# Fused attention and feed-forward kernel: chunk 2's q and k transposed on TensorE, chunk 1 prepared after product 1, attention 1 started ahead of product 2

## The chip, the cores and the metric

The kernel runs on one NeuronCore of a Trainium2 chip. The metric is the device time of one execution in microseconds (us). Before the change three runs gave 260.45, 261.06 and 263.18 us; the median is 261.06.

## The reference, cut to what matters

```python
# q, k, v: (4, 8, 768, 64) float32; three of the eight heads are "retrieval" heads
scores = q @ k.T / 8                      # per batch and head
mask = causal                             # retrieval heads 0, 2, 6
mask = causal & (key < 4 | query - key < 64)   # the five other (streaming) heads
a = softmax(where(mask, scores, -1e9)); attn = a @ v
x = attn.transpose(0, 2, 1, 3).reshape(3072, 512)
h = x @ w_in                              # (512, 2048)
out = maximum(0.01 * h, h) @ w_out        # (2048, 512), float32
```

## The kernel before, in words

The 3072 tokens are cut into eight chunks of 384 (two per batch, `n = 0 .. 7`). A chunk passes through four stages. Its q, k and v come from DRAM by GpSimd's DMAs, cast to bfloat16 on the way (`load`, L78), 256 bytes of DRAM per head and token. Its q and k are transposed so that the head dimension lies on the partitions (`kt`, `qt`). Then comes attention (`Attention`, L276), whose result `xs` is transposed again to `xt`. Then the two feed-forward products: product 1 (`in_slots`, L451) makes `g` from `xt` in 16 ticks of four matmuls and one ScalarE activation, and product 2 (`out_slots`, L463) makes three output tiles from `g` in 16 slots, each tile copied from PSUM by VectorE and stored by SyncE's queue.

There are two ways to transpose. Chunks 0 and 1 do it on TensorE: `prep_pair(n, p)` (L193) transposes one pair of heads with six 128x128 transposes into one PSUM bank, and VectorE copies them out, two halves to `kt` and one tile to `qt`. Chunks from `BY_DMA` = 2 on do it with the DMA crossbar: `prep_dma(n)` (L216) issues six `dma_start_transpose` on SyncE's queue, three for k (from `kz`, a copy of k with zeroed halves) and three for q. The `xt` of chunks 0 to 2 is made on TensorE (`x_t`, L408, three transposes and one ScalarE copy for each pair of heads); from chunk 3 on it is a crossbar transpose issued from `finish` (L404).

The order of each engine's work is the order in which the program is written (`manual_schedule`); nothing is rescheduled. Stages are interleaved by hand: `merge(ms, as_)` (L494) spreads the list `as_` over the list `ms`. Attention is a list of slots; slot t computes the scores of unit t, and the product with v of unit t-2. Product 1 of chunk 0 starts at L542; L543 to L546 put the four pairs of chunk 1 behind its first seven ticks. L551 merges the last five ticks with the first eight slots of attention 1, and then product 2 of chunk 0 with the rest. L560 merges both products of chunk 1 with attention 2. The loop from L563 merges product 1 of chunk n, product 2 of chunk n-1 (from n = 3 on) and attention n+1.

GpSimd's DMAs are issued in program order and use eight completion semaphores in turn, so each issue waits until the DMA issued eight earlier has landed. SyncE's queue is also in program order: vb copies (`v_shift`), crossbar transposes and output stores wait behind each other. PSUM has eight banks: two each for the tags `ph`, `psS` and `po`, one each for `py` and `pt`.

Of the kernel before, what the change touches and what calls it, by code (L numbers as in the profile page):

```python
# [21 lines left out]
def kernel(  # L22
# [13 lines left out]
    B, H, S, D = q.shape  # L36
# [8 lines left out]
    KG = DM // 128  # L45
    NCH = B * (S // CH)

    BY_DMA = 2

    ctx.enter_context(tc.manual_schedule())  # L50
    one = ctx.enter_context(tc.tile_pool(name="one", bufs=1))
# [5 lines left out]
    def bank(tag, shape, dtype):  # L57
        return ps.tile(shape, dtype, name=tag, tag=tag, bufs=BANKS[tag])
# [19 lines left out]
    def load(n, nms="kqv"):  # L78

        b, c = divmod(n, 2)  # L80
        for nm in nms:
            if nm == "k" and n >= BY_DMA:

                for g in range(3):
                    for hh in range(2):
                        nc.gpsimd.dma_start(out=kz[n % 2][:, g, hh::2, D * hh : D * hh + D],  # L86
                                            in_=nat[nm][b, c, :, hh::2, g])
                continue
            if nm != "v":
                cast[nm, n] = rot.tile([128, 3, H, D], BF16, name=f"{nm}b", tag=f"{nm}b", bufs=2)  # L90
            for g in range(3):
                o = va[b % 2][:, 3 * c + g, :, 0:D] if nm == "v" else cast[nm, n][:, g]
                nc.gpsimd.dma_start(out=o, in_=nat[nm][b, c, :, :, g])  # L93

    def load_w(which, i):

        if which == "in":
            c = slice(512 * i, 512 * i + 512)
            nc.gpsimd.dma_start(out=w_in_bf[:, :, c], in_=w_in_r[:, :, c])
        else:  # L100
            c = slice(4 * i, 4 * i + 4)
            nc.gpsimd.dma_start(out=w_out_bf[:, c, :], in_=w_out_r[:, c, :])
# [27 lines left out]
    def zeros(i, c):  # L130
        t = slice(CH * c, CH * c + CH)
        nc.vector.memset(kt[i][64:128, :, 0, t], 0.0)
        nc.vector.memset(kt[i][0:64, :, 1, t], 0.0)

    def zeros_k(i):
        nc.vector.memset(kz[i][:, :, 0::2, D:], 0.0)
        nc.vector.memset(kz[i][:, :, 1::2, 0:D], 0.0)
# [48 lines left out]
    def sink_keys(n, p, hh):  # L186
        b, c = divmod(n, 2)
        h = 2 * p + hh
        if c == 0 and not IS_RETR[h]:
            r = slice(64 * hh, 64 * hh + 64)  # L190
            nc.vector.tensor_copy(ksink[b % 2][r, p, NS * h : NS * h + NS], kt[b % 2][r, p, hh, 0:NS])

    def prep_pair(n, p, tag="pt", eng=("v", "v", "v")):  # L193
        b, c = divmod(n, 2)
        i = b % 2
        if p == 0:
            qts[n] = rot.tile([128, 4, CH], BF16, name="qt", tag="qt", bufs=2)
        pt = bank(tag, [128, 2, 4, 128], BF16)
        for e, nm in enumerate("kq"):
            for g in range(3):  # L200
                nc.tensor.transpose(pt[:, e, g, :], cast[nm, n][:, g, 2 * p : 2 * p + 2, :], ident[:])

        def move(e, dst, src):
            dst = dst.rearrange("p (g t) -> p g t", g=3)
            if e == "v":
                nc.vector.tensor_copy(dst, src)
            else:
                nc.scalar.activation(out=dst, in_=src, func=ACTF.Copy)

        for hh in range(2):  # L210
            r = slice(64 * hh, 64 * hh + 64)
            move(eng[hh], kt[i][r, p, hh, CH * c : CH * c + CH], pt[r, 0, 0:3, :])
            sink_keys(n, p, hh)
        move(eng[2], qts[n][:, p, :], pt[:, 1, 0:3, :])

    def prep_dma(n):  # L216
        b, c = divmod(n, 2)
        i = b % 2
        qts[n] = rot.tile([128, 4, CH], BF16, name="qt", tag="qt", bufs=2)
        for g in range(3):  # L220
            t = slice(128 * g, 128 * g + 128)
            tk = slice(CH * c + 128 * g, CH * c + 128 * g + 128)
            nc.sync.dma_start_transpose(out=kt[i].rearrange("p a e t -> p (a e) t")[:, :, tk],
                                        in_=kz[n % 2][:, g].rearrange("p h d -> p (h d)"))
            nc.sync.dma_start_transpose(out=qts[n][:, :, t], in_=cast["q", n][:, g].rearrange("p h d -> p (h d)"))
# [223 lines left out]
    py = {}  # L449

    def in_slots(n, tags=("ph",)):  # L451
        def tick(t):
            if t == 0:
                gs[n] = rot.tile([128, NG, CH], BF16, name="g", tag="g", bufs=2)
            ph = bank(tags[t % len(tags)], [128, 512], FP32)
            for g in range(KG):
                nc.tensor.matmul(ph[:, 0:CH], lhsT=w_in_bf[:, g, 128 * t : 128 * t + 128],  # L457
                                 rhs=xts[n][:, g, :], start=(g == 0), stop=(g == KG - 1))
            nc.scalar.activation(out=gs[n][:, t, :], in_=ph[:, 0:CH], func=ACTF.Prelu, alpha=0.01)  # L459

        return [lambda t=t: tick(t) for t in range(NG)]

    def out_slots(n, tags=("py", "py", "py"), halves=False):  # L463
        slots = []

        def part(tt, lo, hi, tag, c0, c1):
            if lo == 0:
                py[n] = bank(tag, [128, 512], FP32)
            for ng in range(lo, hi):
                nc.tensor.matmul(py[n][:, 0 : c1 - c0], lhsT=gs[n][:, ng, 128 * tt : 128 * tt + 128],  # L470
                                 rhs=w_out_bf[:, ng, c0:c1], start=(ng == 0), stop=(ng == NG - 1))
            if hi == NG:
                o = rot.tile([128, DM], FP32, name="o", tag="o", bufs=3)
                r0 = CH * n + 128 * tt
                nc.vector.tensor_copy(o[:, 0 : c1 - c0], py[n][:, 0 : c1 - c0])  # L475
                nc.sync.dma_start(out=out[r0 : r0 + 128, c0:c1], in_=o[:, 0 : c1 - c0])

        for tt in range(3):
            if halves and tt == 2:
                slots.append(lambda: part(2, 0, NG, "py", 0, 256))  # L480
                slots.append(lambda: part(2, 0, NG, "psS", 256, 512))
                continue
            lo = 0
            for w in ([3, 3, 3, 3, 4], [3, 3, 3, 3, 4], [3, 3, 3, 3, 2, 2])[tt]:
                slots.append(lambda tt=tt, lo=lo, w=w: part(tt, lo, lo + w, tags[tt], 0, DM))
                lo += w
        return slots

    def run(*lists):
        for l in lists:  # L490
            for f in l:
                f()

    def merge(ms, as_):  # L494

        r, done = [], 0
        for j, m in enumerate(ms):
            want = (j + 1) * len(as_) // len(ms)
            r += as_[done:want] + [m]
            done = want  # L500
        return r + as_[done:]

    def preps(n):
        return [lambda p=p: prep_pair(n, p) for p in range(4)]
# [13 lines left out]
    load(0, "v")  # L518
    load_vb0()
    masks()  # L520
    for i in range(3):
        load_w("in", i)
    load(1, "kq")
    load_w("in", 3)
    load(1, "v")
    for a in ats:
        nc.vector.memset(a[:, :, 1:3, :], 0.0)
    for i in range(4):
# [8 lines left out]
    run(a0[6:])  # L537
    zeros(0, 1)
    nc.vector.memset(ksink[1][:], 0.0)
    zeros_k(0)  # L540
    load(2)
    in0 = in_slots(0, ("ph", "psS"))  # L542
    run(in0[0:7])  # L543
    for p in range(4):
        prep_pair(1, p, ("py", "pt")[p % 2])
        run(in0[7 + p : 8 + p])  # L546
    v_shift(1, nc.sync)
    prep_dma(2)

    a1 = Attention(1, po_tags=("po", "po", "po", "ph")).slots(order=[0, 2, 6, 1, 3, 4, 5, 7])  # L550
    run(merge(in0[11:], a1[:8]) + merge(out_slots(0, ("py", "ph", "py")), a1[8:]))  # L551
    zeros_k(1)
    v_shift(2, nc.sync)
    load(3)
    load(4)
    prep_dma(3)
    v_shift(3, nc.sync)
    for h in range(H):
        sink_keys(2, h // 2, h % 2)
    run(merge(in_slots(1) + out_slots(1, ("py", "ph", "py")), Attention(2).slots()))  # L560
    outs = []

    for n in range(2, NCH):  # L563
        a = []
        if n + 3 < NCH:
            load(n + 3)
        if n + 2 < NCH:
            prep_dma(n + 2)
            v_shift(n + 2, nc.sync)
        if n + 1 < NCH:  # L570

            a = Attention(n + 1, x_dma=True).slots()
            a += [lambda: None] * (len(a) // 5)
        run(merge(merge(in_slots(n), outs) if outs else in_slots(n), a))
        if n + 2 < NCH:
            for h in range(H):
                sink_keys(n + 2, h // 2, h % 2)
        outs = out_slots(n, ("py", "pt", "py")) if n + 1 < NCH else out_slots(n, ("psS", "psS", "py"), True)
    run(outs)


# [33 lines left out]
```

## Time and profile before

| what | us |
|---|---|
| median of three runs | 261.06 |
| the profiled execution | 262.11 |
| its span, first to last instruction | 260.4 |
| TensorE busy in that span | 227.8 |
| ScalarE / VectorE / GpSimd busy | 128.8 / 85.0 / 81.6 |

The profile is of one execution; 1.7 us of its time lie outside the span. Times in rows count from the span's start. PE is TensorE, ACT ScalarE, DVE VectorE, POOL GpSimd; SPq is SyncE's queue of DMA issues. In a view by stretches a row gives the stretch, its length, the busy time and instructions of PE, PEld (weight loads), DVE, ACT and POOL, the granted clock as a share of 2.4 GHz, the mean busy share of the DMA engines (over 1 where transfers of several queues overlap) and GB/s. "[7.21 <-X]" or "idle before <-X" means that the engine stood still and X is what released it. L457 is a matmul of product 1, L470 one of product 2, L329 and L365 scores, L296 the product with v, L201 and L411 transposes.

### The profile page before, as it was taken

What the parts mean: (1) busy time and instruction counts of PE and PEld (TensorE: products, weight loads), DVE (VectorE), ACT (ScalarE), POOL (GpSimd) and SP (SyncE); (2) the same over time, 40 slices, a digit from 0 to 9 for tenths busy, and PEclk for the clock granted to TensorE, in tenths of its full rate; (3) what the DMA queues carried; (4) which work ended last, traced back from release to release, by engine and by line L of the source; (5) the groups of instructions that cost most, each with busy time, mean ns of one, the idle gap of its engine ahead of it and who ended that gap; (6) DMA issues with size and microseconds to landing.
All of it is one profiled execution on the core that took longest, in us unless ns stands there. A gap on an engine that the chain in (4) does not pass through costs nothing.

```text
span 260.4 us, 4912 instructions
## 1 busy us (share of the span) xinstructions
PE 227.8 (87%) x1923; PEld 136.9 (53%) x1948; DVE 85.0 (33%) x247; ACT 128.8 (49%) x276; POOL 81.6 (31%) x111
## 2 busy tenths in 40 slices
PE   1868888980999999927999999999999999999994
PEld 0654554640565567503665566556655665555543
DVE  6883520551134325301341134324421334111111
ACT  2666284540584289712553667555636675333300
POOL 8985633966246672481660000000000000000000
PEclk9999799997699999995999999999999999999999
DMA  9999999999999999999999593348521012111012
GB/s 161 127 191 166 185 233 182 134 125 170 227 141 173 166 195 146 177 127 145 218 154 119 118 134 87 60 95 133 139 73 40 21 38 73 55 40 40 6 77 82
DMA packets 121371, 32.37 MB, mean 124 GB/s; under 512 B 112132, under 2 KB 117508, under 8 KB 121348
## 3 DMA queue, kind: packets, MB, share of 16 engines
q0 software_dynamic: 78352, 13.51, 78.6%
q1 hardware_dynamic: 42896, 18.53, 37.8%
q8 instruction: 15, 0.25, 0.4%
q14 instruction: 8, 0.07, 0.1%
q10 hardware_dynamic: 100, 0.02, 0.0%
HBM read 27.81 MB, written 6.29 MB: 131 GB/s over the span
## 4 chain that ended last, share of the span: by engine, by line
PE 68%; DMA 19%; POOL 8%; issue 2%; DVE 2%; ACT 1%; SPq 0%; POOLq 0%
PE ph L457 27%; PE py L470 17%; PE pt L470 6%; DMA w_out_bf<-in_moe_w_out_dram 6%; PE po L296 5%; PE psS L329 4%; DMA w_in_bf<-in_moe_w_in_dram 4%; PE psS L470 3%; DMA kz<-in_k_dram 3%; POOL va L93 3%; DMA qt<-qb 3%; DMA xt<-xs 2%; PE psS L365 2%; POOL qb L93 2%; PE ph L470 1%
## 5 line engine op out<-in xcount | busy, mean ns | idle before, releaser
L457 PE MATMUL ph<-xt,w_in_bf 128*128 128x384 bf16 x480 | 99.9, 334 | 6.3 <-DMA xt<-xs 6.2
L459 ACT ACTIVATE g<-ph 128x384 bf16<-128x384 f32 x120 | 58.8, 490 | 62.7 <-PE ph L457 62.1
L457 PEld LDWEIGHTS <-w_in_bf 128*128 128x128 bf16 x512 | 47.2, 100 | 35.8 <-issue 6.6
L470 PE MATMUL py<-w_out_bf,g 128*128 128x512 bf16 (+1 forms) x226 | 60.4, 378 | 2.0 <-DMA w_out_bf<-in_moe_w_out_dram 0.8
L470 PEld LDWEIGHTS <-g 128*128 128x128 bf16 x400 | 35.7, 98 | 32.3 <-issue 6.9
L334 ACT ACTIVATE at<-psS 128x384 bf16<-128x384 f32 x81 | 38.8, 490 | 23.4 <-PE psS L329 21.9
L86 POOL DMA_DIRECT2D kz<-in_k_dram x36 | 26.8, 753 | 36.4 <-DMA kt<-kz 18.8
L329 PE MATMUL psS<-qt,kt 128*128 128x384 bf16 (+2 forms) x104 | 27.2, 303 | 7.7 <-DMA qt<-qb 7.2
L475 DVE COPY o<-py 128x512 f32<-128x512 f32 (+1 forms) x15 | 10.1, 672 | 45.8 <-PE py L470 45.8
L93 POOL DMA_DIRECT2D qb<-in_q_dram x24 | 21.3, 906 | 9.2 <-PE psS L329 2.6
L93 POOL DMA_DIRECT2D va<-in_v_dram x24 | 21.3, 906 | 3.9 <-DMA kz<-in_k_dram 2.6
L370 ACT ACTIVATE ats<-psS 128x384 bf16<-128x384 f32 x38 | 18.5, 489 | 5.2 <-PE psS L365 5.1
L329 PEld LDWEIGHTS <-kt 128*128 128x128 bf16 x108 | 10.9, 102 | 18.2 <-issue 10.3
L296 PE MATMUL po<-va,at 128*128 128x65 bf16 x237 | 20.5, 197 | 0.0
L470 PE MATMUL pt<-w_out_bf,g 128*128 128x512 bf16 x72 | 19.8, 379 | 0.4
L296 PEld LDWEIGHTS <-at 128*128 128x128 bf16 x252 | 16.6, 100 | 6.4 <-issue 0.5
L340 DVE TENSOR_TENSOR at<-at,m_caus 128x128 bf16<-128x128 bf16 x24 | 5.4, 224 | 39.3 <-ACT at L334 39.2
L402 DVE TENSOR_TENSOR xs<-po,linv 128x384 bf16<-128x384 f32 x30 | 16.7, 557 | 1.0
L338 DVE TENSOR_TENSOR at<-at,m_caus 128x256 bf16<-128x256 bf16 x24 | 7.0, 292 | 26.5 <-ACT at L334 26.3
L365 PEld LDWEIGHTS <-kt 128*128 128x128 bf16 x240 | 12.7, 102 | 5.5 <-issue 0.3
L296 PEld LDWEIGHTS <-ats 128*128 128x128 bf16 x240 | 11.6, 98 | 3.5 <-DVE ats L377 0.3
L365 PE MATMUL psS<-qt,kt 128*128 128x64 bf16 x228 | 13.3, 197 | 0.0
(97 smaller groups left out, 175.5 us busy)
## 6 DMA issues: line engine op xcount, KB each, us to landing
out_dram<-o SPq DMA_DIRECT2D x23, 256.0 KB, 2.1
qb<-in_q_dram POOLq DMA_DIRECT2D x24, 128.0 KB, 6.2
va<-in_v_dram POOLq DMA_DIRECT2D x24, 128.0 KB, 8.4
kz<-in_k_dram POOLq DMA_DIRECT2D x36, 64.0 KB, 7.8
w_in_bf<-in_moe_w_in_dram POOLq DMA_DIRECT2D x4, 512.0 KB, 8.9
w_out_bf<-in_moe_w_out_dram POOLq DMA_DIRECT2D x4, 512.0 KB, 13.7
vb<-va SPq DMA_DIRECT2D x8, 195.0 KB, 4.9
vb<-va SPq DMA_DIRECT2D x6, 130.0 KB, 5.2
```

The source lines that it names most:

```text
L86: nc.gpsimd.dma_start(out=kz[n % 2][:, g, hh::2, D * hh : D * hh + D], in_=nat[nm][b, c, :, hh::2, g])
L93: nc.gpsimd.dma_start(out=o, in_=nat[nm][b, c, :, :, g])
L296: nc.tensor.matmul(o, lhsT=lhsT, rhs=rhs, start=first, stop=False, skip_group_check=True)
L329: nc.tensor.matmul(s[:, off : off + w], lhsT=kt[i][:, p, hh, 128 * kj : 128 * kj + 128], rhs=qts[n][:, p, lo:CH], start=(j == 0), stop=(j ...
L334: nc.scalar.activation(out=a[:, 0:off], in_=s[:, 0:off], func=ACTF.Exp, scale=SM)
L365: nc.tensor.matmul(s[:, 64 * m : 64 * m + 64], lhsT=kt[i][:, p, hh, k0 : k0 + 128], rhs=qts[n][:, p, 64 * m : 64 * m + 64], start=(m == 0) ...
L370: nc.scalar.activation(out=av_, in_=s[:, 0:CH].rearrange("p (j e f) -> p j e f", j=3, e=2), func=ACTF.Exp, scale=SM)
L402: nc.vector.tensor_tensor(xs[:], po[:, :, :, 0:D], linv.to_broadcast([128, 3, 2, D]), op=ALU.mult)
L457: nc.tensor.matmul(ph[:, 0:CH], lhsT=w_in_bf[:, g, 128 * t : 128 * t + 128], rhs=xts[n][:, g, :], start=(g == 0), stop=(g == KG - 1))
L459: nc.scalar.activation(out=gs[n][:, t, :], in_=ph[:, 0:CH], func=ACTF.Prelu, alpha=0.01)
L470: nc.tensor.matmul(py[n][:, 0 : c1 - c0], lhsT=gs[n][:, ng, 128 * tt : 128 * tt + 128], rhs=w_out_bf[:, ng, c0:c1], start=(ng == 0), stop= ...
L475: nc.vector.tensor_copy(o[:, 0 : c1 - c0], py[n][:, 0 : c1 - c0])
```

## The change

`BY_DMA` becomes 3, so chunk 2's k is loaded as a plain cast (`kb`) and its q and k are transposed on TensorE, by `preps(2)`, merged behind the first tick of product 1 of chunk 1. Attention 3 makes its `xt` on TensorE (`late` is false for it) and has no empty slots at its end any more. The four pairs of chunk 1 come behind tick 12 of product 1 and not behind tick 7; w_in's last quarter is loaded ahead of chunk 1's k and q. Four slots of attention 1 run alone, and the rest is merged with product 2. The zeroing of `kt[1]`'s first half is new, `zeros_k` moves, and `load(3)` is issued one stage earlier in the program. Product 2 of chunk 2 uses the bank `py` for all three tiles, since `pt` is used by attention 3.

```diff
-    BY_DMA = 2
+    BY_DMA = 3
...
-    for i in range(3):
+    for i in range(4):
         load_w("in", i)
-    load(1, "kq")
-    load_w("in", 3)
-    load(1, "v")
+    load(1)
...
-    zeros_k(0)
     load(2)
     in0 = in_slots(0, ("ph", "psS"))
-    run(in0[0:7])
+    run(in0[0:12])
     for p in range(4):
         prep_pair(1, p, ("py", "pt")[p % 2])
-        run(in0[7 + p : 8 + p])
+        run(in0[12 + p : 13 + p])
     v_shift(1, nc.sync)
-    prep_dma(2)
+    zeros(1, 0)
+    zeros_k(1)
+    load(3)
+    zeros_k(0)
 
     a1 = Attention(1, po_tags=("po", "po", "po", "ph")).slots(order=[0, 2, 6, 1, 3, 4, 5, 7])
-    run(merge(in0[11:], a1[:8]) + merge(out_slots(0, ("py", "ph", "py")), a1[8:]))
-    zeros_k(1)
+    run(a1[0:4])
+    run(merge(out_slots(0, ("py", "ph", "py")), a1[4:] + [lambda: None] * 3))
     v_shift(2, nc.sync)
-    load(3)
     load(4)
     prep_dma(3)
     v_shift(3, nc.sync)
-    for h in range(H):
-        sink_keys(2, h // 2, h % 2)
-    run(merge(in_slots(1) + out_slots(1, ("py", "ph", "py")), Attention(2).slots()))
+    in1 = in_slots(1)
+    run(in1[0:1])
+    run(merge(in1[1:] + out_slots(1, ("py", "ph", "py")), preps(2) + Attention(2).slots()))
...
-            a = Attention(n + 1, x_dma=True).slots()
-            a += [lambda: None] * (len(a) // 5)
+            late = n + 1 > 3
+            a = Attention(n + 1, x_dma=late).slots()
+            if late:
+                a += [lambda: None] * (len(a) // 5)
...
-        outs = out_slots(n, ("py", "pt", "py")) if n + 1 < NCH else out_slots(n, ("psS", "psS", "py"), True)
+        outs = out_slots(n, ("py", "pt", "py") if n > 2 else ("py", "py", "py")) if n + 1 < NCH else out_slots(n, ("psS", "psS", "py"), True)
```

SyncE's queue, from the first vb copy (chunk 1's) to the vb copies of chunk 2, with what the change takes out:

```order
 L177 DMA vb_77<-va_75 64x1560
 L178 DMA vb_77<-va_75 64x1560
-L223 DMA_TRANSPOSE kt_74<-kz_82 128x8x128
-L225 DMA_TRANSPOSE qt<-qb 128x4x128
-L223 DMA_TRANSPOSE kt_74<-kz_82 128x8x128
-L225 DMA_TRANSPOSE qt<-qb 128x4x128
-L223 DMA_TRANSPOSE kt_74<-kz_82 128x8x128
-L225 DMA_TRANSPOSE qt<-qb 128x4x128
 L476 DMA out_dram<-o 128x512 x3
 L177 DMA vb_78<-va_76 64x1040
```

The six crossbar transposes of chunk 2 are gone, and the three stores of chunk 0's output (L476) stand right behind chunk 1's vb copies. Further on, the four transposes `xt<-xs` of chunk 3 are gone in the same way.

VectorE, between the last pair of chunk 1 (`qt<-pt`) and the first masks of attention 1 (L340, L338):

```order
 L206 COPY kt_73<-pt 64x384 x2
 L206 COPY qt<-pt 128x384
+L132 MEMSET kt_74 64x4x192
+L133 MEMSET kt_74 64x4x192
+L136 MEMSET kz_83 128x12x32
+L137 MEMSET kz_83 128x12x32
+L136 MEMSET kz_82 128x12x32
+L137 MEMSET kz_82 128x12x32
 L340 TENSOR_TENSOR at<-at,m_caus 128x128
 L338 TENSOR_TENSOR at<-at,m_caus 128x2x128
```

Six fills now stand ahead of attention 1's first mask; two of them (`kt_74`) are new, and the others stood in earlier or later places.

GpSimd's queue, from the first w_in quarter to chunk 2's loads (`kb`, `qb`, `va_75` are chunk 1's on the first lines):

```order
-L99 DMA w_in_bf<-in_moe_w_in_dram 128x4x512 x3
+L99 DMA w_in_bf<-in_moe_w_in_dram 128x4x512 x4
 L93 DMA kb<-in_k_dram 128x8x64 x3
 L93 DMA qb<-in_q_dram 128x8x64 x3
-L99 DMA w_in_bf<-in_moe_w_in_dram 128x4x512
 L93 DMA va_75<-in_v_dram 128x8x64 x3
 L102 DMA w_out_bf<-in_moe_w_out_dram 128x4x512 x4
-L86 DMA kz_82<-in_k_dram 128x4x64 x6
+L93 DMA kb<-in_k_dram 128x8x64 x3
 L93 DMA qb<-in_q_dram 128x8x64 x3
```

Chunk 1's k and q stand behind one more quarter of w_in, and chunk 2's k comes as three DMAs into `kb` in the place of six into `kz`.

## Rows read from the trace of the kernel before

**Rows 1.** Waits of TensorE: who, for what: us in total, times, longest

```profile
PE psS L329 <- DMA qt<-qb: 7.2, 1, 7.2
PE ph L457 <- DMA xt<-xs: 6.2, 4, 3.6
PE py L470 <- DMA w_out_bf<-in_moe_w_out_dram: 0.8, 1, 0.8
```

**Rows 2.** Three stretches: busy time by engine, granted clock, DMA share, GB/s

```profile
65.00:70.00 5.00, 4.73 (x19) 2.51 (x20) 0.52 (x2) 2.23 (x5) 1.11 (x2) 0.59 1.39 251
120.00:125.00 5.00, 5.00 (x32) 2.81 (x31) 1.26 (x4) 1.92 (x5) 1.50 (x2) 0.63 1.82 161
143.00:260.40 117.40, 112.39 (x883) 65.82 (x897) 30.77 (x81) 56.25 (x121) 0.00 (x0) 1.00 0.31 73
```

**Rows 3.** TensorE's timeline about the first stall: start, us, instruction [idle before]

```profile
57.25 0.81 PE L457 MATMUL ph<-xt,w_in_bf 128*128 128x384 bf16 x4
65.27 0.48 PE L329 MATMUL psS<-qt,kt 128*128 128x384 bf16 x1 [7.21 <-DMA qt<-qb]
70.08 0.34 PE L365 MATMUL psS<-qt,kt 128*128 128x64 bf16 x6
```

**Rows 4.** The same about the second stall

```profile
91.98 0.33 PE L329 MATMUL psS<-qt,kt 128*128 128x384 bf16 x1
...
111.03 0.33 PE L329 MATMUL psS<-qt,kt 128*128 128x384 bf16 x1
...
118.80 1.48 PE L470 MATMUL py<-w_out_bf,g 128*128 128x512 bf16 x3
...
124.77 0.81 PE L470 MATMUL py<-w_out_bf,g 128*128 128x512 bf16 x3
```

**Rows 5.** TensorE's timeline, last pair of chunk 1, then a tick

```profile
31.93 0.33 PE L201 MATMUL pt<-ident,kb 128*128 128x128 bf16 x3
...
32.27 0.81 PE L457 MATMUL ph<-xt,w_in_bf 128*128 128x384 bf16 x4
32.92 0.33 PE L329 MATMUL psS<-qt,kt 128*128 128x384 bf16 x1
```

**Rows 6.** VectorE's timeline: fills of kt and kz, copies of one pair

```profile
19.70 0.70 DVE L132 MEMSET kt<- 64x768 uint32 x1 [0.22 <-issue]
...
32.47 0.72 DVE L206 COPY kt<-pt 64x384 bf16<-64x384 bf16 x2
33.21 0.36 DVE L206 COPY qt<-pt 128x384 bf16<-128x384 bf16 x1
...
58.17 0.38 DVE L136 MEMSET kz<- 128x384 uint32 x1
```

**Rows 7.** Costliest groups of the page: busy, mean ns of one, idle before

```profile
L334 ACT ACTIVATE at<-psS 128x384 bf16<-128x384 f32 x81 | 38.8, 490 | 23.4 <-PE psS L329 21.9
L475 DVE COPY o<-py 128x512 f32<-128x512 f32 (+1 forms) x15 | 10.1, 672 | 45.8 <-PE py L470 45.8
```

**Rows 8.** TensorE's timeline: chunk 1's q arrives; product 2 starts; w_out arrives

```profile
27.59 0.23 PE L201 MATMUL py<-ident,qb 128*128 128x128 bf16 x1 [0.29 <-DMA qb<-in_q_dram]
...
39.94 0.81 PE L470 MATMUL py<-w_out_bf,g 128*128 128x512 bf16 x2
```

**Rows 9.** GpSimd's queue: issues released by w_in's last quarter and by crossbar transposes

```profile
30.39 0.74 POOL L86 DMA_DIRECT2D kz<-in_k_dram  x1 [1.61 <-DMA w_in_bf<-in_moe_w_in_dram]
...
109.42 1.49 POOL L86 DMA_DIRECT2D kz<-in_k_dram  x2 [1.21 <-DMA kt<-kz]
```

**Rows 10.** SyncE's queue: crossbar transposes of chunks 3, 4 (k first, q last)

```profile
62.01 2.32 SPq L223 DMA_TRANSPOSE kt<-kz  x1
...
73.85 2.19 SPq L225 DMA_TRANSPOSE qt<-qb  x1
...
93.33 1.46 SPq L223 DMA_TRANSPOSE kt<-kz  x1
...
104.23 2.01 SPq L225 DMA_TRANSPOSE qt<-qb  x1
```

## The prediction

> **What bounds the kernel now.** I read the waits of TensorE first, then the clock by stretches, then TensorE's timeline about the longest waits, then the queues behind them. TensorE is busy for 112.39 of the last 117.40 us at full clock [rows 2], so from 143 us on there is little to win. Before that two waits stand out: 7.2 us for chunk 2's crossbar transposes (`qt`), and 6.2 us in four pieces for chunk 3's (`xt`) [rows 1]. Each costs more than its length, since after each the granted clock is low: 0.59 and 0.63 in the five microseconds behind [rows 2], which is a stretch partly at 1.2 GHz after TensorE had stood still. The change takes away both transfers. So its gain is what the two places cost, less the work that TensorE takes over, less what is late next.
>
> **Unit prices.** A tick of product 1 takes 0.65 us (32.27 to 32.92), and a group of three 128-column transposes 0.17 (two groups, 31.93 to 32.27) [rows 5]. A score of 384 columns has as many columns as such a group, so 0.17 too; a matmul of product 2 has a third more columns than one of a tick's four, so 0.22.
>
> **What goes, first place.** The first tick of chunk 1 starts at 57.25 and would be over at 57.90; the score behind it starts at 65.27 [rows 3]: 7.37 us lost. From there to 70.08 [rows 3] stand 16 matmuls of product 1 and two scores, at full clock 2.6 + 0.33 = 2.93 us of the 4.81: 1.9 lost. Together 9.3 us. After the change nothing waits for a crossbar here: chunk 2's loads are issued from 30.39 on [rows 9], 27 us ahead of that tick.
>
> **What goes, second place.** The score at 111.03 and a tick would end at 111.85; the next work starts at 118.80 [rows 4]: 6.95 lost. From 118.80 to 124.77 [rows 4] stand six matmuls of product 2, two ticks, two scores, the sink scores (four matmuls of 256 columns, 0.44) and a few short products with v (0.2): 3.6 us at full clock of 5.97, so 2.4 lost. Together 9.35 us. Sum of both: 18.65 us.
>
> **What is added on TensorE.** Eight groups of transposes for chunk 2 and four for `xt` of chunk 3, 12 x 0.17 = 2.0 us, all on the path, since TensorE is full there. The four `xt` copies go to ScalarE. In the loop of attention 3 it then has 16 + 21 + 4 = 41 activations, at 0.49 us each [rows 7] 20.1 us, just the loop's own length. They overlap at their ends when they stand back to back, so I cost the four at nothing; without that cover they would be 4 x 0.49 = 2.0 us.
>
> **What the four pairs of chunk 2 wait for.** All use the one bank `pt`, so a pair's transposes wait until VectorE has copied the pair before: 0.72 + 0.36 [rows 6], and some 0.2 for small sink copies and hand-over (my estimate), 1.3 us. Between the pairs stand one tick, two ticks, one tick: 0.65, 1.30 and 0.65 us of cover. Waits of 0.6 + 0 + 0.6 = 1.2 us. Bounds: 0, if attention's idle slack takes them, and 2.0, if each of the three waits 0.65.
>
> **Three tiles of chunk 2's product 2 on one bank.** A tile's first matmul waits for VectorE's copy of the tile before, 0.67 us [rows 7]; between them lie a tick (0.65) and a score. I take 0.3 in all; bounds 0 and 2 x 0.67 = 1.3.
>
> **Chunk 0's products and attention 1.** Chunk 1's q was in at 27.59 [rows 8]; w_in's last quarter was in by 30.39, when it released a load [rows 9]. Put ahead of k and q, it makes them up to 2.8 us later, but 12 ticks now run before they are needed, and not 7. Pair 0 ends at about 30.4. What follows, four ticks and three pairs, took from 27.65 to 32.92 [rows 5] before (partly at the low clock), so it ends at 35.7 with all 16 ticks done. Then five slots of attention 1 run without cover, one exponential of 0.49 [rows 7] each: 38.2. Product 2 so starts 1.7 us before 39.94 [rows 8]. In its stretch it gets three more slots of attention (some 0.8 us); it waits for the first mask, because six fills stand ahead of it on VectorE (two at 0.70 and a gap of 0.2, four at 0.38 [rows 6], 3.4 us behind the last pair's copies, so free at 39.7 where the masked product is due at 38.8: 0.9); and having started earlier it meets w_out's last quarter, for which it waited 0.8 before [rows 1], some 0.7 longer. -1.7 + 0.8 + 0.9 + 0.7 = +0.7. Because these waits partly hide each other I take +0.5. Bounds: -1.5, if the two waits are hidden, and +3, if k and q come 2.8 later and nothing makes up for it.
>
> **Sum.** -18.65 + 2.0 + 1.2 + 0.3 + 0.5 = -14.6 us. Against the profiled execution: 262.11 - 14.6 = 247.5. That execution lies 1.05 us above the median of the runs, 261.06, so for a median I predict 246.5. With the bounds of the added terms (-1.5 + 0 + 0, +3 + 2.0 + 1.3, and 2.0 if the copies aren't hidden) the sum's own range is 244 to 251, and I hold 244 to 249.5 for likely, because the upper ends would have to fall together.
>
> **What is late next.** Attention 3 starts at 91.98 [rows 4] before and, by the terms up to there (-9.3 + 1.4 + 1.2 + 0.5), at 85.8 after. It needs chunk 3's crossbar transposes, whose last issue was over at 73.85 + 2.19 = 76.04 [rows 10] and comes no later now, with six transposes fewer ahead of them. Attention 4 needs chunk 4's. Before, they were issued from 93.33, 1.35 us after attention 3's start, and their last k was in by 109.42 [rows 9], q by 111.03, when the score did not wait: 16.1 to 17.7 us. Started at 87.1 they are in at 103.2 to 104.8; the score is due 19.05 + 0.7 after 85.8, at 105.5. The slack is 0.7 to 2.3 us: thin. A rule speaks on this. The Trainium skill, Advanced Engine Details and Errata, section X-Bar Transpose (TRN2), says that "TRN2 transpose DMAs are as fast as regular DMAs", 350 to 400 GB/s. By it chunk 4's six (three of 256 KB, three of 128 KB) would need some 3 us, an estimate from that page, the slack would be 15 us and rival A below would have no chance. The trace doesn't agree: the issues alone go from 93.33 to 104.23 + 2.01 = 106.24 [rows 10], so I leave A its chance.
>
> **Rivals.**
> A. Chunk 4's transposes are late. For it: the thin slack, and that loads and crossbar share the DMA engines, busy share 1.4 to 1.8 in such stretches [rows 2]. Against: fewer transposes ahead. Chunk 3's issues took 14 us (62.01 to 76.04), chunk 4's 12.9 [rows 10]; with two to three microseconds more the score waits 1 to 3, and then the clock costs about 2 as in both places above: 246.5 + 4.5 = 251, 250 to 253.
> B. The first stage loses more: waiting for q, then for the first exponentials, then for w_out lowers the clock through product 2's first tile. For it: both long waits of the profile did. Against: w_out's wait of 0.8 didn't. Half clock over 16 matmuls of 0.22 adds 3.5: 250.
> C. The other side: the loads set the pace, and the stalls return one stage later. The place is the first score of attention 3, waiting for chunk 3's transposes. They cost nothing until 85.8; every microsecond later adds one, and from 85.8 + 14.6 = 100.4 on the kernel is slower than before: 261 to 265 with the low clock behind. For it: POOL's loads wait for transposes [rows 9], so one late thing makes the next late. Against: before, with six more transposes in the same queue, the last issue was over at 76.04 [rows 10], nearly 10 us ahead.
>
> **How the numbers follow.** My forecast 0.62, A 0.19, B 0.11, C 0.08, half of it within 1% and half slower. One per cent, 2.6 us, is about what a measurement of this kernel can tell from no change. Faster by over 1% (under 258.4) are the forecast, A and B: 0.92; within 1% 0.04; slower 0.04. The range goes from 243.5, just under the sum's low end, to 252.5, through most of A.
>
> **What would show it.** Right: no wait for `qt` or `xt` among TensorE's waits before 110 us; product 1's second tick of chunk 1 right behind the first; clock 1.00 from about 36 us on; attention 3's first score near 86, attention 4's near 105.5, and the last 117 us as before. Three short waits of TensorE at L201 for VectorE near 60 us would show the `pt` term; a wait of a product with v for VectorE near 39 us the fills. Wrong: a wait of L329 for a crossbar transpose at 86 (C) or 105 (A), or a clock under 0.9 between 38 and 57 us (B).

## The result, and the profile after

The changed kernel takes 248.68 us in the median of four runs (247.94 to 248.99); the kernel before, run beside it on the same chip, 261.55 us. The ratio is 0.950, with a 95% interval of 0.944 to 0.956: faster by 12.9 us. The forecast was 246.5, with 243.5 to 252.5 as its range. The profiled execution took 248.99 us and its span is 247.3, against 262.11 and 260.4 before: the span lost 13.1 us where the sum had 14.6. (A ratio leaves out runs that lie more than 1.5% above the fastest of the same kernel: one of the kernel before, two of e1 and one of e7.)

First TensorE's waits in the changed kernel, those that the prediction speaks of and the new ones (who, for what: us in total, times, longest):

```profile
PE pt L201 <- DVE qt L206: 2.5, 3, 1.1
PE py L201 <- DMA qb<-in_q_dram: 2.0, 3, 0.7
...
PE po L296 <- DVE at L340: 1.0, 1, 1.0
PE py L470 <- DMA w_out_bf<-in_moe_w_out_dram: 0.7, 1, 0.7
```

The two rows at the head of [rows 1], 7.2 us for `qt` and 6.2 for `xt`, have no successor. What is new is small: the three waits of the pairs of chunk 2 for VectorE (line L201 for L206), one of a product with v for a masked `at`, and two of 0.3 and 0.4.

Then the stretches that answer to [rows 2], with the first stage ahead of them (columns as there: stretch, length, busy time of PE, PEld, DVE, ACT, POOL, granted clock, DMA share, GB/s):

```profile
30.00:35.00 5.00, 4.14 (x24) 2.59 (x25) 2.19 (x7) 0.88 (x2) 3.76 (x6) 0.66 1.74 184
60.00:65.00 5.00, 3.10 (x25) 1.68 (x24) 3.60 (x11) 1.82 (x4) 3.03 (x5) 1.00 1.67 205
65.00:70.00 5.00, 4.45 (x40) 3.02 (x41) 2.42 (x8) 3.08 (x8) 3.64 (x5) 1.00 2.00 162
116.00:121.00 5.00, 5.00 (x61) 3.21 (x60) 2.17 (x7) 3.03 (x7) 2.88 (x4) 1.00 1.45 222
130.00:247.30 117.30, 113.40 (x900) 65.92 (x898) 30.80 (x81) 56.41 (x121) 0.00 (x0) 0.99 0.33 76
```

Where the clock was 0.59 and 0.63 it is 1.00. Only behind the pieces of waiting for chunk 1's q, from 31.0 to 34.4 us, is it still at the lower of its two levels, as it was for as long before, from 28.2 us on. From chunk 4's first tick to the end both kernels take about the same: 114.73 us before (from 145.67) and 114.48 after.

TensorE's timeline at the places of [rows 3, 4, 8], and the start of chunk 4's product 1 in both kernels, after and then before (start, us, instruction [idle before]):

```profile
31.09 0.29 PE L201 MATMUL py<-ident,qb 128*128 128x128 bf16 x1 [0.62 <-DMA qb<-in_q_dram]
...
36.38 0.33 PE L329 MATMUL psS<-qt,kt 128*128 128x384 bf16 x1
...
38.65 0.81 PE L470 MATMUL py<-w_out_bf,g 128*128 128x512 bf16 x3
...
40.60 0.27 PE L296 MATMUL po<-va,at 128*128 128x65 bf16 x3 [0.97 <-DVE at L340]
...
57.68 1.46 PE L457 MATMUL ph<-xt,w_in_bf 128*128 128x384 bf16 x8
...
59.32 0.81 PE L457 MATMUL ph<-xt,w_in_bf 128*128 128x384 bf16 x4
61.24 0.34 PE L201 MATMUL pt<-ident,kb 128*128 128x128 bf16 x3 [1.10 <-DVE qt L206]
...
63.46 0.34 PE L201 MATMUL pt<-ident,kb 128*128 128x128 bf16 x3 [0.41 <-DVE qt L206]
...
65.55 0.34 PE L201 MATMUL pt<-ident,kb 128*128 128x128 bf16 x3 [0.94 <-DVE qt L206]
...
67.20 0.33 PE L329 MATMUL psS<-qt,kt 128*128 128x384 bf16 x1
...
87.48 0.33 PE L329 MATMUL psS<-qt,kt 128*128 128x384 bf16 x1
...
107.49 0.33 PE L329 MATMUL psS<-qt,kt 128*128 128x384 bf16 x1
...
132.82 0.81 PE L457 MATMUL ph<-xt,w_in_bf 128*128 128x384 bf16 x4
```

```profile
145.67 0.81 PE L457 MATMUL ph<-xt,w_in_bf 128*128 128x384 bf16 x4
```

With these the span divides into five parts. The part up to chunk 1's product 1 grew from 57.25 to 57.68. From there to attention 3's first score it was 34.73 us (57.25 to 91.98, [rows 3, 4]) and is 29.80: -4.93. Attention 3's loop, 19.05 [rows 4], is 20.01: +0.96. From attention 4's first score to chunk 4's first tick it was 34.64 (111.03 to 145.67) and is 25.33: -9.31. The rest is 114.73 and 114.48, -0.25. The sum is 0.43 - 4.93 + 0.96 - 9.31 - 0.25 = -13.1.

### The profile page after: what moved, and what is told of

The parts are those of the page before. It is cut to its first block, busy times and chain, and to the rows that moved or that the text cites. A ratio compares the mean times of both kernels' runs of the same rounds, so it can differ in the third digit from the quotient of the medians.

```text
span 247.3 us, 4993 instructions
## 1 busy us (share of the span) xinstructions
PE 226.4 (92%) x1984; PEld 136.7 (55%) x1984; DVE 92.2 (37%) x261; ACT 130.4 (53%) x280; POOL 80.3 (32%) x108
## 4 chain that ended last, share of the span: by engine, by line
PE 76%; DMA 11%; POOL 6%; DVE 4%; issue 1%; ACT 1%; POOLq 0%
PE ph L457 27%; PE py L470 21%; PE po L296 6%; DMA w_out_bf<-in_moe_w_out_dram 6%; PE pt L470 6%; DMA w_in_bf<-in_moe_w_in_dram 5%; PE psS L329 4%; PE psS L470 4%; PE ph L470 3%; PE psS L365 2%; POOL va L93 2%; PE psS L309 2%; DVE o L475 1%; POOL qb L93 1%; POOL w_out_bf L102 1%
## 5 line engine op out<-in xcount | busy, mean ns | idle before, releaser
L457 PE MATMUL ph<-xt,w_in_bf 128*128 128x384 bf16 x480 | 97.6, 327 | 0.1
L470 PE MATMUL py<-w_out_bf,g 128*128 128x512 bf16 (+1 forms) x256 | 66.4, 372 | 1.3 <-DMA w_out_bf<-in_moe_w_out_dram 0.7
L457 PEld LDWEIGHTS <-w_in_bf 128*128 128x128 bf16 x512 | 46.4, 98 | 30.1 <-issue 1.0
L470 PEld LDWEIGHTS <-g 128*128 128x128 bf16 x400 | 35.4, 97 | 27.6 <-issue 2.3
L86 POOL DMA_DIRECT2D kz<-in_k_dram x30 | 22.5, 770 | 23.1 <-DMA kt<-kz 18.7
L475 DVE COPY o<-py 128x512 f32<-128x512 f32 (+1 forms) x16 | 10.8, 674 | 43.7 <-PE py L470 43.7
L329 PE MATMUL psS<-qt,kt 128*128 128x384 bf16 (+2 forms) x104 | 26.4, 295 | 0.6 <-ACT g L459 0.4
L470 PE MATMUL pt<-w_out_bf,g 128*128 128x512 bf16 x64 | 17.1, 379 | 0.0
L329 PEld LDWEIGHTS <-kt 128*128 128x128 bf16 x108 | 10.5, 100 | 9.9 <-issue 2.1
L340 DVE TENSOR_TENSOR at<-at,m_caus 128x128 bf16<-128x128 bf16 x24 | 5.3, 222 | 27.6 <-ACT at L334 27.3
L365 PEld LDWEIGHTS <-kt 128*128 128x128 bf16 x240 | 12.4, 101 | 5.4 <-issue 0.2
L365 PE MATMUL psS<-qt,kt 128*128 128x64 bf16 x228 | 13.1, 195 | 0.0
L338 DVE TENSOR_TENSOR at<-at,m_caus 128x256 bf16<-128x256 bf16 x24 | 7.0, 291 | 15.7 <-ACT at L334 15.5
```

What stands on the lines that cost most here:

```text
L329: nc.tensor.matmul(s[:, off : off + w], lhsT=kt[i][:, p, hh, 128 * kj : 128 * kj + 128], rhs=qts[n][:, p, lo:CH], start=(j == 0), stop=(j ...
L365: nc.tensor.matmul(s[:, 64 * m : 64 * m + 64], lhsT=kt[i][:, p, hh, k0 : k0 + 128], rhs=qts[n][:, p, 64 * m : 64 * m + 64], start=(m == 0) ...
```

## The experiments

Each is the changed kernel with one edit, unless said; e9 builds on e3, and e8 on e9. Of some edits only the main lines are shown, with "..." for the rest. Two open questions set them: whether the two places are worth what the sum gave them, and what the terms on the other side of the sum (pairs, fills, first stage) really cost. Ratios are to the kernel before, whose medians beside these runs were 261.23 us (e1, e2, e3, e5) and 261.94 (e4, e7, e9, e8).

**e1: only chunk 3's `xt` goes back to the crossbar.** The prediction's reckoning (the second stall is an affair of the crossbar alone) stands against a rival: it was partly an echo of chunk 2's six transposes.

```diff
-            late = n + 1 > 3
+            late = n + 1 > 2
```

> The changed kernel, but attention 3's xt goes by the crossbar again (with its empty slots); chunk 2 stays on TensorE. Theory P (each of the two places paid for itself): product 1 of chunk 3 waits for xt again, 6 to 7 us and 2.4 us of low clock, less 0.7 us of transposes: about 248.7 + 8.5 = 257 us, and a wait of L457 for xt of 5 us or more. Rival R (one cause: chunk 2's crossbar transposes held up the loads and all that followed, the xt wait was its echo): chunk 4's transposes are over at 98 us in the changed kernel, so SyncE's queue is free for xt, and the wait is under 1.5 us: 248 to 250 us.

Measured: 250.1, 252.61, 254.67 and 254.8 us, median 253.64; the ratio 0.962 (0.956 to 0.969) goes by the lower two. The profiled run is the one at 252.61, 3.6 above the changed kernel's. Its wait, and the two matmuls of the first tick that wait:

```profile
PE ph L457 <- DMA xt<-xs: 3.4, 2, 2.4
```

```profile
107.45 0.32 PE L457 MATMUL ph<-xt,w_in_bf 128*128 128x384 bf16 x1 [1.03 <-DMA xt<-xs]
...
110.17 0.32 PE L457 MATMUL ph<-xt,w_in_bf 128*128 128x384 bf16 x1 [2.39 <-DMA xt<-xs]
```

The same four transfers that held TensorE for 6.2 us [rows 1] hold it for 3.4 when chunk 2's are away, and behind them the clock is 0.50 from 110.9 to 114.3 us. So the stall belongs to them, but nearly half of its length went with the rest of the change. Neither expectation was met: the wait is neither over 5 us nor under 1.5, and the median lies between the two times. Where the 2.8 us went is seen in SyncE's queue, before and in e1:

```profile
107.62 5.58 SPq L404 DMA_TRANSPOSE xt<-xs  x4
```

```profile
98.37 5.52 SPq L404 DMA_TRANSPOSE xt<-xs  x4
```

The four issues stand behind chunk 4's six transposes, whose issues took 12.9 us before [rows 10] and 8.9 in e1 (88.14 to 96.99). So they began 3.6 us ahead of their tick before (111.2) and 7.6 us ahead in e1 (105.94); the four themselves were no faster, 11.8 us from the first issue to the end of the last wait against 10.9. The rival is thus right in so far as the second stall was partly made by what stood ahead of it in the queue. That it is chunk 2's part of the change that sped those six up is argued: e5 leaves out the first stage, and e2, which puts chunk 2's transposes back, has chunk 4's slow again (see rival A below).

**e2: only chunk 2's q and k go back to the crossbar.**

```diff
-    BY_DMA = 3
+    BY_DMA = 2
...
+    prep_dma(2)
...
-    run(merge(in1[1:] + out_slots(1, ("py", "ph", "py")), preps(2) + Attention(2).slots()))
+    run(merge(in1[1:] + out_slots(1, ("py", "ph", "py")), Attention(2).slots()))
```

> The changed kernel, but chunk 2's k and q go by the crossbar again, issued behind chunk 1's vb copies as before; xt of chunk 3 stays on TensorE. Theory P: the first score of chunk 2 waits again for qt, some 6 to 7 us, and 1.9 us of low clock follow; 1.4 us of transposes and 2.9 us of waits for the bank pt go: 248.7 + 8.5 - 4.3 = 253 us, with a later start of attention 3. Rival R: the same first wait, and behind it chunk 4's crossbar transposes late by several us again (the score of chunk 4 or xt waits), so 256 us or more. A wait under 2 us at the first score of chunk 2 would be against both: 244 to 246 us.

Measured: 253.19 us, ratio 0.970 (0.966 to 0.974). (The edit also puts back the fills and sink copies that belong to the crossbar way.) The stall and the low clock are back: TensorE's wait, its timeline, and the stretch at half clock, which begins within the wait and outlasts it by 4.1 us:

```profile
PE psS L329 <- DMA qt<-qb: 6.5, 1, 6.5
```

```profile
57.19 1.46 PE L457 MATMUL ph<-xt,w_in_bf 128*128 128x384 bf16 x8
65.19 0.48 PE L329 MATMUL psS<-qt,kt 128*128 128x384 bf16 x1 [6.53 <-DMA qt<-qb]
```

```profile
62.50:69.30 6.80, 4.11 (x14) 2.01 (x15) 0.36 (x2) 1.85 (x4) 3.11 (x4) 0.50 1.47 238
```

From chunk 1's first tick to chunk 2's it takes 34.36 us (to 91.55), the changed kernel 29.96 (57.68 to 87.64): this place is worth 4.4 us net, as transposes and waits on TensorE take back about half of the 9.3. Undone one at a time the two parts cost less than the 12.9 us that the change gave, and the timelines show where the difference lies. From attention 3's first score to chunk 4's first tick, the second place, it took 53.69 us before (91.98 to 145.67) and takes 45.34 in the changed kernel (87.48 to 132.82): -8.35. In e2 it takes 45.34 as well (91.39 to 136.73), and in e1 49.77 (86.73 to 136.50). So undone alone the second part costs 4.4 us there and not 8.35: the two parts help each other, as the shorter `xt` wait of e1 says too. The size of this, some 3.9 us, is uncertain by about 2, since e1's runs spread by 4.7; its slowest run, 2.2 above the profiled one, would leave 1.7 if all of that lay here. By the ratios alone it would be open: e2 costs 5.2 us, and e1 3.2 by its lower two runs or 5.5 by the median of all four, and the gap to 12.9, 4.5 or 2.2, is uncertain by 2.5. The first stage gave none of it (e5 below).

**e3: the pairs of chunk 2 use the banks `py` and `pt` in turn.** The prediction holds three waits of 1.2 us in all for the price of one bank; the trace after says 2.5 to 2.95.

```diff
-        return [lambda p=p: prep_pair(n, p) for p in range(4)]
+        return [lambda p=p: prep_pair(n, p, ("py", "pt")[p % 2]) for p in range(4)]
```

> The changed kernel, but chunk 2's four pairs use the banks py and pt in turn (py is free until product 2 of chunk 1). Theory: the three pair-to-pair waits, 2.45 us by the waits and 2.95 us from the end of the tick to the first transpose, go, and TensorE is ahead by that to the end: 246.0 us, 2.3 to 2.9 below the changed kernel. Rival: what is saved is lost again later, because VectorE's copies (4 x 1.66 us) or chunk 3's transposes are late next: 248 to 249 us, and a new wait of 1.5 us or more at L329.

Measured: 246.83 us, ratio 0.945 (0.941 to 0.948), span 245.5. No wait of L201 for VectorE is left; chunk 2's product 1 starts at 84.94 and not 87.64, 2.7 us sooner. Of these the span keeps 1.8 (245.5 against 247.3). Its interval overlaps the changed kernel's, so that it is faster rests on the timeline. Most of what is lost again is a new wait, for chunk 4's `xt` on the crossbar:

```profile
PE ph L457 <- DMA xt<-xs: 0.7, 1, 0.7
```

**e4: the sink copies move behind the copy of q.** A sink copy takes four columns of `kt` to a small tile for the streaming heads. VectorE's timeline in the changed kernel, about the first pair and in the third:

```profile
59.52 0.73 DVE L206 COPY kt<-pt 64x384 bf16<-64x384 bf16 x2 [0.94 <-PE pt L201]
60.28 0.53 DVE L191 COPY ksink<-kt 64x4 bf16<-64x4 bf16 x1
60.82 0.36 DVE L206 COPY qt<-pt 128x384 bf16<-128x384 bf16 x1
...
64.39 0.16 DVE L191 COPY ksink<-kt 64x4 bf16<-64x4 bf16 x1
```

```diff
             move(eng[hh], kt[i][r, p, hh, CH * c : CH * c + CH], pt[r, 0, 0:3, :])
-            sink_keys(n, p, hh)
         move(eng[2], qts[n][:, p, :], pt[:, 1, 0:3, :])
+        for hh in range(2):
+            sink_keys(n, p, hh)
```

> The changed kernel, but a pair's small sink copies (L191, 4 columns) come behind the copy of q, so that they no longer stand before the bank pt is free. Theory: my 1.3 us for a pair's copies was too small because the sink copies take 0.16 to 0.53 us on the way (1.66 us in all); without them the cycle is about 1.2 us, the three waits fall from 2.45 to some 1.1 us, and the time by 1.0 to 1.4: 247.4 us. Rival: the copies that are left set the cycle anyway, and the waits stay above 2 us: 248.7.

Measured: the waits of L201 fall from 2.5 to 1.1 us, chunk 2's product 1 starts at 86.04 (1.6 sooner), the span is 245.6. The median is 247.63, ratio 0.948 (0.943 to 0.952); this interval overlaps the changed kernel's, so that it is faster rests on the timeline. Its waits, and VectorE at the first pair:

```profile
PE pt L201 <- DVE qt L206: 1.1, 2, 0.6
```

```profile
59.33 0.72 DVE L206 COPY kt<-pt 64x384 bf16<-64x384 bf16 x2 [0.94 <-PE pt L201]
60.09 0.36 DVE L206 COPY qt<-pt 128x384 bf16<-128x384 bf16 x1
60.48 0.17 DVE L191 COPY ksink<-kt 64x4 bf16<-64x4 bf16 x1
```

The pairs' waits are thus set by VectorE: 1.66 us of copies for the first pair (59.52 to 61.18), of which the 4-column sink copy is 0.53; behind q it is 0.17 and out of TensorE's way. How much of the 1.6 is the move is not shown, since in e7 below the sink copies of the first two pairs are as short without it.

**e5: the first stage as before** (w_in's last quarter behind k and q, pairs behind tick 7, product 1's end merged with attention 1), the rest changed.

```diff
...
-    run(in0[0:12])
+    run(in0[0:7])
...
-    run(a1[0:4])
-    run(merge(out_slots(0, ("py", "ph", "py")), a1[4:] + [lambda: None] * 3))
+    run(merge(in0[11:], a1[:8]) + merge(out_slots(0, ("py", "ph", "py")), a1[8:]))
```

> The changed kernel with the first stage as before: w_in's last quarter behind chunk 1's k and q, pairs of chunk 1 behind ticks 7 to 10, attention 1 merged with the last five ticks and then with product 2. Theory: this part of the change was worth nothing (product 1 of chunk 1 started at 57.25 before and 57.68 after): 248.7 within 0.7 us, product 1 of chunk 1 starting at 57 to 58. Rival: it is what keeps the clock up and w_out's wait short now that six fills stand on VectorE; without it product 1 of chunk 1 starts 1.5 to 3 us later: 250 to 252 us.

Measured: 248.75 us, ratio 0.952 (0.949 to 0.955); chunk 1's product 1 starts at 57.33, against 57.68. That part of the change is worth nothing by itself.

**e7: the six fills stand ahead of the pairs of chunk 1**, so that the first mask need not wait for them.

```diff
+    zeros(1, 0)
+    zeros_k(1)
+    zeros_k(0)
...
     for p in range(4):
...
```

> The changed kernel, but the six fills stand ahead of chunk 1's pairs, where VectorE is idle. Theory (waits of the first stage hide each other): the wait of 1.0 us of L296 for the mask goes, the wait for w_out's last quarter grows from 0.7 to about 1.7, product 1 of chunk 1 still starts at 57.4 to 57.8, and the time is 248.7 within 0.4. Rival: the fills were on the path by themselves: start at 56.8, 247.8 us.

Measured: 248.61 us in the median of six runs (one of them at 301.75), ratio 0.949 (0.945 to 0.954). The 0.97 for `at` is gone, and the wait for w_out grew from 0.7 to 1.8:

```profile
PE py L470 <- DMA w_out_bf<-in_moe_w_out_dram: 1.8, 2, 1.0
```

Chunk 1's product 1 starts at 57.41, only 0.27 sooner. What TensorE doesn't wait for on VectorE it waits for on w_out's load.

The trace shows one more thing. The sink copies of chunk 2's first two pairs take 0.17 us here, in the same place and order in which they took 0.53 and 0.48, and TensorE waits 1.7 us for the pairs and not 2.5:

```profile
60.00 0.17 DVE L191 COPY ksink<-kt 64x4 bf16<-64x4 bf16 x1
```

```profile
60.60 0.34 PE L201 MATMUL pt<-ident,kb 128*128 128x128 bf16 x3 [0.74 <-DVE qt L206]
```

Chunk 2's product 1 so starts at 86.68, 0.96 us sooner than in the changed kernel (87.64), of which 0.27 come from the first stage.

**e9: e3, and chunk 4's `xt` on TensorE too** (`late = n + 1 > 4`).

> e3 (two banks for chunk 2's pairs), and attention 4's xt on TensorE too. Theory: with two banks TensorE is 2.7 us ahead at chunk 2 but loses 0.9 of it at product 1 of chunk 4, where xt of chunk 4 is now the next thing late (0.7 us of wait); four groups of transposes cost 0.7, so little or nothing is gained: 246 to 247 us. Rival: that wait varies from run to run as in e1 and is longer in the median; then 245 to 246 us.

Measured: 246.20 us, ratio 0.941 (0.937 to 0.945), span 244.6 against 245.5 of e3; the intervals overlap. The 0.7 for `xt` is gone. Chunk 4's first tick starts at 130.46, no sooner than in e3 (130.12), but e3's last matmul of that tick waits until 131.50, and the score behind it comes at 131.10 here and at 131.66 there: 0.6 us.

**e8: e9 with a thinner first stage**: the fills early, k and q loaded ahead of w_in's last quarter, pairs back to back, and attention 1 spread over product 2 with most of it early.

```diff
...
+    o0 = out_slots(0, ("py", "ph", "py"))
+    run(merge(o0[:4], a1[:20]) + merge(o0[4:], a1[20:]))
...
```

> e9 and a new first stage: chunk 1's k and q ahead of w_in's last quarter again, 12 ticks, the four pairs together, the last four ticks, then 20 slots of attention 1 spread over the first four slots of product 2 (those that do not need w_out's last quarter), and the rest over the other twelve; fills early, chunk 2's vb copies ahead of the stores. Theory: the first stage is bound by w_out's last quarter, in at 45 us, and by what is left to do then; with attention 1 nearly done by then product 1 of chunk 1 starts at 54 to 55 and not at 57.7: 243 to 244.5 us. Rival: TensorE runs so thin between 33 and 45 us that the clock falls, or xs and g wait for ScalarE, and the start stays at 57 or later: 246 to 248 us.

Measured: 244.87 us (244.38 to 245.79), ratio 0.936 (0.931 to 0.940): the best version, ahead of both kernels. Chunk 1's product 1 starts at 56.34; expected were 54 to 55. Earlier quarters of w_out are still waited for (0.73 and 0.34 us), but the last one no longer sets the time: it was in by 45.01, when it released a load, and the fourth and fifth slots of product 2, of which the fifth is the first to need it, start at 46.48 without a wait, behind 20 slots of attention 1:

```profile
45.01 1.83 POOL L93 DMA_DIRECT2D va<-in_v_dram  x2 [1.65 <-DMA w_out_bf<-in_moe_w_out_dram]
```

```profile
46.48 1.46 PE L470 MATMUL py<-w_out_bf,g 128*128 128x512 bf16 x6
```

From 33.55, the first score, to 46.48 TensorE was busy for 10.16 of 12.93 us. The clock is at full speed in every stretch up to 200 us:

```profile
15.00:30.00 15.00, 11.96 (x122) 7.74 (x119) 9.69 (x26) 8.86 (x19) 10.41 (x13) 1.00 1.69 185
30.00:60.00 30.00, 26.68 (x251) 16.18 (x253) 12.39 (x36) 14.90 (x33) 19.12 (x24) 1.00 1.76 187
60.00:200.00 140.00, 137.44 (x1276) 84.54 (x1294) 50.57 (x150) 87.40 (x194) 37.37 (x46) 1.00 1.21 126
```

And with everything earlier, attention 4's first score now does wait for chunk 4's crossbar:

```profile
104.09 0.32 PE L329 MATMUL psS<-qt,kt 128*128 128x384 bf16 x1 [0.76 <-DMA qt<-qb]
```

## Why the prediction was right, and which terms were off

**The two places.** Right, in kind and size. At the second, -9.35 was worked out and -9.31 measured, so the term of +0.3 beside it, three tiles on the bank `py`, cost nothing: no wait of L470 for VectorE stands among TensorE's waits. At the first, adding the transposes and waits back to the -4.93 gives -4.93 - 1.36 - 2.95 = -9.24, against -9.3. About 4.3 of the 18.65 is the low clock. That it goes with the stall, and not with the work at these places, is shown by e2 and e1, where the wait and the clock of 0.50 return together. What the prediction didn't have is that the second stall hangs on the first part of the change too (8.35 us net for both, 4.4 for `xt` alone in e1); its sum didn't need it, since both went.

**The waits on the bank `pt`.** This is the mis-sized term: 1.2 us predicted, 2.95 measured. From the end of the tick at 59.97 (59.32 + 0.65) to the next pair at 61.24 are 1.27 us, then 0.58 and 1.10, counted in the same way; the prediction had 0.6, 0 and 0.6. The step that failed is "some 0.2 for small sink copies and hand-over". From the end of a pair's transposes to the next pair's is 1.92 us (59.32 to 61.24), 1.66 of them copies, where 1.3 was assumed, so that even the two ticks (1.30) don't cover it. The upper bound of 2.0, three waits of 0.65, was too low as well: the two waits behind one tick took 1.27 and 1.10. e3 takes the waits away and moves chunk 2's product 1 by 2.7 us, e4 takes the sink copies out of the cycle and moves it by 1.6. The difference of 1.75 is more than the 1.5 by which the sum missed the span. Of the 2.2 us between 246.5 and the measured median, the other 0.7 is that the profiled execution lies 0.31 above its median, where 1.05 was carried over from the kernel before.

**The first stage.** +0.5 predicted, +0.43 measured, the terms partly by luck. The first score of attention 1 is at 36.38 (35.7 predicted, the transposes of pair 0 having waited for q until 31.09), product 2 at 38.65 (38.2), a gain of 1.29 on [rows 8] and not 1.7. The fills cost 0.97 (0.9 predicted). w_out cost 0.74, no more than before [rows 1], where 0.7 longer was predicted. That such waits hide each other was put as a reason for taking +0.5; e7 shows it. The low clock of 31.0 to 34.4 seems to be hidden in the same way: one of the four runs has a mean granted clock of 1.0, so hardly any such stretch, and took 248.74 us, between the others.

**The copies on ScalarE and attention 3's loop.** +0.7 predicted, +0.96 measured: 0.68 for transposes, and the rest is of the size of two new waits, 0.30 for a masked `at` (L338) and 0.23 for `xs`. No wait for a copy of ScalarE stands in that loop, and its 42 instructions there keep ScalarE busy for 17.42 of the 20.01 us, less than 42 x 0.49 = 20.6, so they do overlap and the four copies at nothing were right.

**Rival A, chunk 4's transposes late.** It didn't come, but the slack was not 0.7 to 2.3 us. SyncE's and GpSimd's queues in the changed kernel, at the answer to [rows 9, 10]:

```profile
88.90 1.29 SPq L223 DMA_TRANSPOSE kt<-kz  x1
...
96.28 1.40 SPq L225 DMA_TRANSPOSE qt<-qb  x1
```

```profile
84.06 2.65 POOL L93 DMA_DIRECT2D va<-in_v_dram  x3
94.05 1.50 POOL L86 DMA_DIRECT2D kz<-in_k_dram  x2 [7.35 <-DMA kt<-kz]
...
99.76 1.48 POOL L86 DMA_DIRECT2D kz<-in_k_dram  x2 [1.24 <-DMA kt<-kz]
```

From the first issue to the last k in are 10.9 us (88.90 to 99.76), where the sum took over the 16.1 of before [rows 9, 10]; the score at 107.49 had 7.7 us to spare for k. GpSimd issued no load from 86.71 to 94.05: those of q and v were ahead, and its next one waits for a `kz` that these transposes free. So the transposes met fewer transfers. In e2, with the loads later, the same six took 17.8 us (92.75 to 110.54). The stretches of these transposes, changed kernel and then e2:

```profile
88.90:99.80 10.90, 10.90 (x136) 7.55 (x135) 3.56 (x12) 10.11 (x26) 3.02 (x5) 1.00 1.56 179
```

```profile
92.70:110.60 17.90, 17.36 (x208) 11.68 (x205) 6.91 (x24) 15.73 (x39) 7.42 (x11) 1.00 1.74 159
```

Five issues of loads stand in the shorter stretch and eleven in the longer; the six more are q and v at its head. The other traces agree. Where the last of these q and v issues ended 1.0 to 2.8 us ahead of the first transpose (the changed kernel, e1, e4, e5, e7), the six took 10.5 to 12.1 us; where it ended 1.1 behind it (e3), 13.4; and where it ended 3.0 to 6.8 us behind it (before, e2, e8, e9), 16.1 to 18.4. This orders all ten traces by the loads; that the loads are the cause is still argued, as no run had the transposes alone. The rule of the Trainium skill weighed in the prediction (Advanced Engine Details and Errata, X-Bar Transpose (TRN2)) made this some 3 us, an estimate from that page; 10.5 is the shortest measured (e1 and e5), so the traces don't agree with it for transposes beside other transfers. The step that failed is thus taking over the duration of before without asking what the loads beside it would do. A's mechanism exists: in e8 the score is due 4.2 us sooner (103.33 and not 107.49), the transposes take 18.2 us (84.58 to 102.76 for k), and it waits 0.76 us, without the clock behind it.

**Rivals B and C.** B: the clock did fall in the first stage, but behind the waits for q and for 3.4 us, as before; the waits of 0.97 and 0.74 in product 2 left it alone. C: attention 3's first score came at 87.48 without a wait, where 85.8 was predicted (the 1.75 of the pairs), and chunk 3's last crossbar issue was over at 72.4, 15 us ahead.

**The bounds.** Two of them don't follow from their parts. With both waits hidden the first stage's term is -1.7 + 0.8 = -0.9 and not -1.5. And the sum's own range, counted from the median, goes from 242.9 to 252.7; its 244 to 251 has the low end from the profiled execution and the high end from the median without the 2.0 for the copies. The measured 248.68 lies in either.

## What to carry to other kernels

The long stalls of TensorE here cost their length and a stretch at the lower clock behind them, so price both from the timeline: count what stands in the slow stretch, and take it at full speed. When a transfer is replaced by work on the engine that waited, the copies that empty its one PSUM bank can be the next limit, as here; add up every instruction of that cycle, the four-column ones too, and give the pairs two banks. Durations of transfers are not constants: ask what will be in the queues beside them, and undoing two edits one at a time can show less than both gave together.

## What the runs showed of the hardware that was not expected

The same kind of 64x4 sink copy took 0.53 and 0.48 us behind the two `kt` copies of a pair, 0.16 and 0.17 in the pair where one stands behind each `kt` copy, 0.35 in the fourth pair, and 0.17 behind the q copy (e4). In e7 it took 0.17 in the first two pairs, in the order of the changed kernel and with GpSimd's issues beside it (58.30 to 62.80) as there, so neither the order nor these issues explain it. Why is open.

Waits of 0.4 to 1.1 us with work between them, 2.5 us in all from 59.97 to 65.55, left the clock at 1.00, although TensorE was busy only 3.10 of the 5 us from 60 on; in e2 a single wait of 6.5 us (58.66 to 65.19) had the clock at 0.50 from 62.5 to 69.3.
